# A new listed order for the first part of a linear-attention and two-layer MLP kernel, and two attention stages in some passes of block 2

## The chip, the cores and the metric

The kernel runs on one core of one Trainium2 chip. The metric is the device time of one execution in microseconds, as the median of three runs.

## The reference

Gated linear attention over 4 batches, 8 heads, 768 steps and a head width of 48, then two MLPs over the 3,072 tokens (width 384, hidden width 2,048), all in fp32:

```python
for t in range(S):
    state = alpha[:, :, t, :, None] * state + np.einsum('bhd,bhe->bhde', k[:, :, t], v[:, :, t])
    y[:, :, t] = np.einsum('bhd,bhde->bhe', q[:, :, t], state)
x = y.transpose(0, 2, 1, 3).reshape(B * S, H * D)
h = x @ w_in                                   # layer 1
g = np.where(h >= 1, h, np.where(h <= -1, 0.0, (h + 1) ** 2 / 4))
x = g @ w_out
h = x @ w_in2                                  # layer 2
g = h * np.clip(h + 3.0, 0.0, 6.0) / 6.0
out = g @ w_out2
```

## The kernel before

**Tiling.** Tokens lie along the free axis. There are 12 groups of 256 tokens, each with two halves of four heads: 24 attention units. Two groups make a block of 512 tokens; six blocks go through layer 1 and then through layer 2. The hidden width is cut into 16 steps f of 128. For each f, `mm1` makes a tile ph (3 x 3 matmuls of 128x128 by 128x512, because every fp32 operand is split into a high fp32r part and a low rest), ACT and DVE make the gate g from it, and `mm2` adds three output tiles po. Three ph buffers exist, one set of po, two buffers of ps_att for the attention, two x tiles and one more for block 2 (`turns`). The second product of a step is issued two steps behind the first (LAG).

**An attention unit** has stages that the listed order names by words: L and V load its data; p (scan of the gates), r (reciprocal), s (second scan), k (keys), R and Rc (queries) prepare it on DVE and ACT; T transposes the keys on TensorE and kt copies them; S makes the scores, m masks them on DVE; ST makes the chunk states, h, st and z sum and carry them; O makes the outputs into a ps_att tile, xc copies its high part into x on ACT, xl subtracts the low part on DVE (the last reader of the tile), mv moves 16 rows of each half head from a stage tile into x by six DMAs on POOL's queue, after both units of a group; gd is a range check on ACT that also ends the use of the loaded tile.

**Weights** come as 64-bit words of 768 KB a step: LW loads, ca (ACT), cb, cc, cd (DVE) turn them into fp32 in place, hi (ACT) and lo (DVE) split them. Words A, g, mx, gh, gl, B are the parts of a step of the MLP: A0_f is f of the first part of block 0, done with whole fp32 weights (`mm1_whole`, six recorded matmuls), A1 is block 1, A2 the rest of block 0; oc copies the three po tiles out. W n issues n filler matmuls that nobody reads.

**Order.** The string ORDER is run word by word, and a dependency added by hand keeps each engine's instructions in just that order: TensorE, DVE, ACT, POOL and SP (which issues the loads) are five queues that each run in the list's order. The list holds units 0 to 11, the preparation of unit 12, and the MLP up to block 0's last steps. Behind it (lines 753 to 804) a Python loop emits blocks 2 to 5 of layer 1 and all of layer 2. There the order on each engine is left to the scheduler that the program is compiled with. In layer 1 each pass f emits one `prep_step` (a third of a unit's preparation) and one `att_step` (a quarter of a unit: T and kt; S and m; ST, h, st and z; O, xc and gd, with xl, mv and the loads of the unit after next behind them). A block's four units are due before the block begins; blocks 2, 3 and 4 have 16 passes and so 16 attention stages each, units 12 to 23 in all. Blocks in the code are counted from 0.

The words L, T and so on are bound in `fns`; `load_qkv` places units 2, 3, 6 and 7 in weight tiles that are not used yet, and the others in a pool of two.

Of the kernel before, what the change touches and what calls it, by code (L numbers as in the profile page):

```python
# [38 lines left out]
ORDER = """
p0 r0 s0 L2 p1 k0 r1 T0 s1 W1 kt0 L3 ST0 k1 R1 T1 h0 Rc1 p2 st0 S1 kt1 z0 m1 ST1 p3 W8 LW1 R0 h1 Rc0 LW0 r3  # L40
st1 S0 s3 gd0 O1 m0 LW2 W1 xc1 k3 ca1 O0 r2 ca0 R3 W6 L4 cb1 xc0 z1 s2 Rc3 mv0 ca2 S3 k2 gd1 T2 m3 V2 W1 kt2
L5 R2 ST2 cc1 Rc2 T3 h2 kt3 p4 S2 st2 V3 ST3 m2 LW3 h3 O2 R4 st3 LW5 r4 s4 xc2 O3 Rc4 W1 k4 xc3 V4 cb0 ca3
S4 mv2 LW4 cc0 ca5 T4 m4 W2 kt4 V5 cd0 ST4 LW7 cb2 hi0 cd1 A0_0 ca4 cc2 LW6 hi1 cd2 sxh p5 A0_1 LW10 g0_0 z2
h4 cb3 A0_2 cc3 LW8 g0_1 mx0_0 cd3 gd4 LW9 B0_0 mx0_1 cb5 st4 z3 r5 s5 g0_2 A0_3 k5 gd3 mx0_2 cb4 O4 cc4 L7
g0_3 cd4 B0_1 cc5 ca7 cd5 gd2 B0_2 V6 mx0_3 xc4 L6 R5 Rc5 p7 ca6 S5 r7 hi2 s7 T5 hi3 L8 A0_5 R7 kt5 k7 Rc7
p6 ca8 A0_4 g0_5 m5 r6 ca9 s6 S7 g0_4 k6 ST5 m7 B0_3 ca10 mx0_4 mx0_5 h5 T6 R6 st5 B0_4 cb6 Rc6 cc6 gd5 cd6
kt6 O5 cb7 cc7 ST6 V7 xc5 xl4 L9 xl5 T7 h6 A0_6 mv4 kt7 lo0 st6 cd7 hi4 z6 ST7 lo1 gd6 lo2 S6 g0_6 h7 A0_7
m6 st7 mx0_6 hi6 z7 O7 p8 gd7 O6 V9 r8 xc7 s8 LW12 B0_5 g0_7 xl7 lo3 xc6 V8 mx0_7 B0_6 hi5 LW14 xl6 hi7 k8
mv6 ca12 lo6 LW13 B0_7 R8 lo4 Rc8 ca14 lo5 LW15 S8 oc0 cb9 cb8 A1_0 m8 LW11 ca13 cc8 A1_1 g1_0 lo7 cd8 A1_2
g1_1 mx1_0 cc9 A1_3 gh1_0 mx1_1 hi8 gl1_0 g1_2 lo8 B1_0 cd9 gh1_1 mx1_2 T8 gl1_1 gh1_2 A1_5 kt8 gl1_2 hi9  # L50
cb10 cc10 g1_3 ST8 cd10 B1_1 h8 hi10 mx1_3 st8 lo9 B1_2 gh1_3 z8 lo10 gd8 gl1_3 A1_4 ca11 cb12 cb11 g1_5
cc11 O8 cb13 A1_6 g1_4 mx1_5 L10 cc13 cd13 gh1_5 B1_3 ca15 mx1_4 gl1_5 gh1_4 V10 A1_7 xc8 gl1_4 cd11 g1_6
cc12 B1_4 g1_7 mx1_6 sxl A1_8 gh1_6 mx1_7 hi11 B1_5 gl1_6 gh1_7 lo11 g1_8 gl1_7 B1_6 cd12 mx1_8 hi12 p9 B1_7
gh1_8 gl1_8 r9 B1_8 s9 R9 A1_10 k9 Rc9 cb14 cc14 A1_11 g1_10 cd14 lo12 T9 mx1_10 hi13 A1_9 cb15 gh1_10 lo13
kt9 gl1_10 hi14 A1_13 cc15 g1_9 cd15 S9 lo14 ST9 mx1_9 hi15 m9 gh1_9 A1_12 gl1_9 h9 g1_11 B1_9 lo15 p10
g1_12 B1_10 mx1_11 R10 gh1_11 mx1_12 A1_14 st9 gl1_11 g1_13 z9 xl8 B1_11 r10 s10 gh1_12 gd9 O9 gl1_12 mx1_13
g1_14 B1_12 L11 k10 gh1_13 mx1_14 A1_15 gl1_13 gh1_14 Rc10 gl1_14 V11 xc9 B1_13 g1_15 xl9 mv8 p11 B1_14
mx1_15 r11 gh1_15 s11 A2_8 gl1_15 k11 B1_15 g2_8 R11 A2_9 oc1 mx2_8 gh2_8 A2_10 g2_9 gl2_8 B2_8 g2_10 mx2_9
S10 gh2_9 mx2_10 T10 gh2_10 m10 A2_12 kt10 Rc11 gl2_10 gl2_9 ST10 g2_12 T11 h10 B2_9 mx2_12 gd10 kt11 B2_10
gh2_12 st10 gl2_12 O10 ST11 V12 xc10 L12 xl10 A2_11 h11 st11 S11 g2_11 A2_13 m11 gd11 mx2_11 O11 p12 gh2_11  # L60
A2_14 V13 xc11 gl2_11 L13 xl11 g2_13 r12 mv10 B2_11 s12 g2_14 mx2_13 B2_12 k12 R12 gh2_13 Rc12 gl2_13 A2_15
mx2_14 gh2_14 gl2_14 g2_15 mx2_15 gh2_15 gl2_15 B2_13
"""
# [828 lines left out]
```

## Time and profile before

| | us |
|---|---|
| median of three runs (971.74 to 974.24) | 973.2 |
| profiled execution | 977.22 |
| its span, first to last instruction | 975.4 |
| TensorE busy / DVE busy / ACT busy | 930.7 / 532.3 / 530.7 |
| mean granted clock of TensorE | 0.976 |

Engines are written PE (TensorE), PEld (its weight loads), DVE, ACT, POOL and SP; SPq and ACTq are the queues that issue DMAs. Times count from the first instruction of the span. L120 is line 120 of the kernel; `ph<-x,w` is a tile written from two others by the program's names, with trailing numbers left out. A releaser is what ended the idle time before an instruction. The granted clock is given as a share of 2.4 GHz.

### The profile page before, as it was taken

The numbers are of one execution on the slowest core, as the hardware profiler recorded it, in microseconds if no ns is written. First come the engines' busy times: TensorE is split into PE (matmuls) and PEld (weight loads), VectorE is DVE, ScalarE is ACT, GpSimd is POOL, SyncE is SP. The second block draws the span as 40 slices with busy tenths as digits, with TensorE's granted clock in tenths as the row PEclk, the third lists the DMA queues.
The fourth block names the chain that finished last, engine by engine and source line by source line (L and its number), as shares of the span: only waits on it lengthen the run. The fifth ranks groups of instructions, "written<-read, shape, count | busy, mean of one in ns | idle before, by whom it ended". The sixth has DMA issues, their size and how long they took to land.

```text
span 975.4 us, 14259 instructions
## 1 busy us (share of the span) xinstructions
PE 930.7 (95%) x5786; PEld 736.0 (75%) x5790; DVE 532.3 (55%) x856; ACT 530.7 (54%) x855; POOL 39.5 (4%) x88
## 2 busy tenths in 40 slices
...
DMA packets 18026, 69.33 MB, mean 71 GB/s; under 512 B 3360, under 2 KB 3680, under 8 KB 15520
## 3 DMA queue, kind: packets, MB, share of 16 engines
...
q10 hardware_dynamic: 608, 0.62, 0.2%
q14 instruction: 27, 0.22, 0.1%
...
## 4 chain that ended last, share of the span: by engine, by line
PE 85%; DMA 5%; DVE 5%; ACT 3%; issue 1%; POOL 0%; SPq 0%; ACTq 0%; DVEq 0%
PE po L161 37%; PE ph L120 37%; PE ph L128 3%; PE ps_att L462 2%; DMA qkv_sb<-in_wgt 2%; PE ps_att L509 2%; PE ps_att L436 2%; PE ps_att L419 1%; DMA qkv_sb<-in_qkv 1%; PE po L134 1%; DMA x<-stage 1%; DVE w L113 1%; DMA xf<-stage 1%; DMA w<-in_qkv 1%; DVE R L446 1%
## 5 line engine op out<-in xcount | busy, mean ns | idle before, releaser
L161 PE MATMUL po<-g,w 128*128 128x512 f32 x1656 | 412.8, 393 | 0.0
L120 PE MATMUL ph<-x,w 128*128 128x512 f32 x1512 | 380.5, 397 | 12.2 <-DVE t L150 7.3
L161 PEld LDWEIGHTS po<-g,w 128*128 128x128 f32 x1656 | 308.7, 188 | 65.3
L120 PEld LDWEIGHTS ph<-x,w 128*128 128x128 f32 x1512 | 287.9, 191 | 74.1 <-DVE t L150 8.6
L786 DVE TENSOR_TENSOR g<-t,g 128x512 fp32r<-128x512 f32 x160 | 110.2, 691 | 95.0 <-ACT g L153 94.6
L153 ACT ACTIVATE g<-t 128x512 fp32r<-128x512 f32 x160 | 100.6, 631 | 104.6 <-DVE t L152 62.4
L152 DVE SCALAR_TENSOR_TENSOR t<-t,ph 128x512 f32<-128x512 f32 x96 | 66.1, 689 | 160.7 <-ACT t L145 160.7
L145 ACT ACTIVATE t<-ph,half 128x512 f32<-128x512 f32 x96 | 66.2, 689 | 158.1 <-PE ph L120 156.9
L140 ACT ACTIVATE t<-ph,half 128x512 f32<-128x512 f32 x96 | 65.7, 685 | 69.9 <-PE ph L120 61.8
L150 DVE TENSOR_TENSOR t<-t,ph 128x512 f32<-128x512 f32 x64 | 43.3, 681 | 47.8 <-ACT t L142 47.4
L142 ACT ACTIVATE t<-t 128x512 f32<-128x512 f32 x96 | 60.1, 630 | 2.3
L141 ACT ACTIVATE t<-t 128x512 f32<-128x512 f32 x96 | 60.1, 630 | 2.2
L120 PE MATMUL ph<-turns,w 128*128 128x512 f32 x144 | 36.3, 397 | 0.0
L550 POOL DMA_DIRECT2D x<-stage x48 | 24.0, 506 | 275.9 <-DVE rec L381 80.7
L374 DVE TENSOR_TENSOR_SCAN qkv_sb<-qkv_sb,zero 128x256 f32<-128x256 f32 x40 | 25.4, 677 | 16.1 <-DMA qkv_sb<-in_qkv 16.1
L446 DVE TENSOR_TENSOR R<-ps_att,mask 64x512 int32<-64x512 int32 x40 | 27.5, 688 | 11.0 <-PE ps_att L436 10.3
L462 PEld LDWEIGHTS ps_att<-qkv_sb,kt 64*64 64x64 f32 (+1 forms) x576 | 21.7, 142 | 15.1 <-issue 9.9
L462 PE MATMUL ps_att<-qkv_sb,kt 64*64 64x48 f32 (+1 forms) x576 | 25.9, 232 | 6.1 <-ACT kt L424 2.5
L120 PEld LDWEIGHTS ph<-turns,w 128*128 128x128 f32 x144 | 27.0, 188 | 6.2
L485 ACT ACTIVATE st<-sh 64x384 f32<-64x384 f32 x48 | 24.9, 519 | 7.7 <-DVE sh L478 6.6
L436 PEld LDWEIGHTS ps_att<-R,qkv_sb 64*64 64x64 f32 x640 | 21.4, 139 | 9.8 <-issue 5.5
L388 DVE TENSOR_TENSOR_SCAN qkv_sb<-qkv_sb,rec,zero 128x256 f32<-128x256 f32 x40 | 27.9, 739 | 0.7
...
## 6 DMA issues: line engine op xcount, KB each, us to landing
...
qkv_sb<-in_wgt SPq DMA_DIRECT2D x16, 768.0 KB, 4.2
w<-in_wgt SPq DMA_DIRECT2D x10, 768.0 KB, 9.5
st<-in_vst SPq DMA_DIRECT2D x44, 128.0 KB, 2.8
w<-in_qkv SPq DMA_DIRECT2D x4, 768.0 KB, 7.8
x<-in_wgt SPq DMA_DIRECT2D x4, 768.0 KB, 10.0
...
```

Source lines behind the costliest of these rows:

```text
L120: nc.tensor.matmul(ph, w[:, a, 0, j * P:(j + 1) * P], x[:, b, j], start=(i == 0), stop=(i == 3 * KD - 1))
L140: nc.scalar.activation(t, ph, AF.Relu, scale=-0.5, bias=half)
L141: nc.scalar.activation(t, t, AF.Relu, scale=-1.0, bias=1.0)
L142: nc.scalar.activation(t, t, AF.Square)
L145: nc.scalar.activation(t, ph, AF.Relu, scale=1.0 / 6.0, bias=half)
L150: nc.vector.tensor_tensor(out=t, in0=t, in1=ph, op=ALU.max)
L152: nc.vector.scalar_tensor_tensor(out=t, in0=t, scalar=1.0, in1=ph, op0=ALU.min, op1=ALU.mult)
L153: nc.scalar.activation(g[:, 0], t, AF.Copy)
L161: nc.tensor.matmul(po[m], w[:, a, 1, m * P:(m + 1) * P], g[:, b], start=(first and i == 0), stop=(last and i == 2))
L436: nc.tensor.matmul(ps[o0:o0 + C, r * NCH + c, :], n["kh"][p0:p0 + C, r, ks], R[p0:p0 + C, h, r, cs], start=True, stop=True,)
L462: nc.tensor.matmul(ps[C * h:C * h + C, c, r, :], n["kt"][k0:P, 2 * r + 1 - c // 2, C * h:C * h + C], n["v"][k0:P, 1 - c // 2, 2 * r + h, : ...
L786: nc.vector.tensor_tensor(out=g[:, 1], in0=tt, in1=g[:, 0].bitcast(F32), op=ALU.subtract)
```

## The change

The string ORDER is replaced by another with the same work and 35 fillers in eight places instead of 20 in seven. The loads of units 0, 1, 2, 3, 6 and 7 become three words each: Lp (the gates, 512 KB), Lk (the keys, 256 KB) and Lq (queries and values, 448 KB); before, unit 0 was loaded in those three parts, unit 1 whole and units 2, 3, 6 and 7 in two parts. The loads of the first two units, which stood ahead of the list, are words of it, and V0 and V1 are issued from SP instead of ACT. The tile of reciprocals is cut from a constant with four places instead of a pool of two. In the loop behind the list, passes 3, 7, 11 and 15 of block 2 emit two attention stages and two preparation steps instead of one. Of ORDER the diff below shows the lines that are spoken of further on.

```diff
 ORDER = """
-p0 r0 s0 L2 p1 k0 r1 T0 s1 W1 kt0 L3 ST0 k1 R1 T1 h0 Rc1 p2 st0 S1 kt1 z0 m1 ST1 p3 W8 LW1 R0 h1 Rc0 LW0 r3
...
-S4 mv2 LW4 cc0 ca5 T4 m4 W2 kt4 V5 cd0 ST4 LW7 cb2 hi0 cd1 A0_0 ca4 cc2 LW6 hi1 cd2 sxh p5 A0_1 LW10 g0_0 z2
-h4 cb3 A0_2 cc3 LW8 g0_1 mx0_0 cd3 gd4 LW9 B0_0 mx0_1 cb5 st4 z3 r5 s5 g0_2 A0_3 k5 gd3 mx0_2 cb4 O4 cc4 L7
-g0_3 cd4 B0_1 cc5 ca7 cd5 gd2 B0_2 V6 mx0_3 xc4 L6 R5 Rc5 p7 ca6 S5 r7 hi2 s7 T5 hi3 L8 A0_5 R7 kt5 k7 Rc7
-p6 ca8 A0_4 g0_5 m5 r6 ca9 s6 S7 g0_4 k6 ST5 m7 B0_3 ca10 mx0_4 mx0_5 h5 T6 R6 st5 B0_4 cb6 Rc6 cc6 gd5 cd6
-kt6 O5 cb7 cc7 ST6 V7 xc5 xl4 L9 xl5 T7 h6 A0_6 mv4 kt7 lo0 st6 cd7 hi4 z6 ST7 lo1 gd6 lo2 S6 g0_6 h7 A0_7
-m6 st7 mx0_6 hi6 z7 O7 p8 gd7 O6 V9 r8 xc7 s8 LW12 B0_5 g0_7 xl7 lo3 xc6 V8 mx0_7 B0_6 hi5 LW14 xl6 hi7 k8
-mv6 ca12 lo6 LW13 B0_7 R8 lo4 Rc8 ca14 lo5 LW15 S8 oc0 cb9 cb8 A1_0 m8 LW11 ca13 cc8 A1_1 g1_0 lo7 cd8 A1_2
...
-kt9 gl1_10 hi14 A1_13 cc15 g1_9 cd15 S9 lo14 ST9 mx1_9 hi15 m9 gh1_9 A1_12 gl1_9 h9 g1_11 B1_9 lo15 p10
-g1_12 B1_10 mx1_11 R10 gh1_11 mx1_12 A1_14 st9 gl1_11 g1_13 z9 xl8 B1_11 r10 s10 gh1_12 gd9 O9 gl1_12 mx1_13
...
+Lp0 Lk0 Lp1 p0 Lq2 r0 s0 Lq0 p1 Lq1 k0 Lk1 R0 T0 r1 Lp2 Lk2 Rc0 s1 kt0 S0 R1 ST0 Lq3 k1 Rc1 m0 W4 Lp3 Lk3 p2
...
+O2 m3 ca4 p4 O3 xc2 gd2 W9 r4 s4 V4 xc3 V5 hi0 mv2 k4 Lq6 R4 T4 cb4 W2 LW3 kt4 p5 Rc4 ST4 cb1 S4 LW5 h4 cc1
+gd4 W7 m4 st4 Lp6 Lk6 cd1 ca3 O4 r5 hi1 A0_0 cb2 L8 cc2 xc4 ca5 xl4 cd2 sxh A0_1 p6 LW7 g0_0 cb5 s5 A0_2
+g0_1 V6 mx0_0 LW6 p8 B0_0 ca7 mx0_1 g0_2 r8 LW10 cb3 cc3 B0_1 ca6 mx0_2 LW9 cd3 hi2 k5 hi3 A0_3 z3 R5 gd3
+LW8 cc4 Rc5 cd4 ca9 B0_2 Lp7 Lk7 cc5 g0_3 cd5 R6 Lq7 T5 ca8 mx0_3 S5 kt5 r6 p7 Rc6 A0_4 ca10 R7 r7 Rc7 s7
...
+LW13 hi5 O7 z7 mx0_5 gd7 p9 T8 V9 B0_5 xc7 R9 LW11 kt8 xl7 g0_6 lo2 mv6 ST8 lo5 LW12 g0_7 mx0_6 S8 h8 B0_6
+m8 st8 Rc9 z8 mx0_7 gd8 lo0 O8 hi6 r9 B0_7 s9 L10 hi4 ca13 k9 ca11 lo4 A1_0 oc0 lo6 V10 cb9 LW15 cb10 A1_1
...
+cd10 A1_8 gl1_5 hi10 xl8 g1_7 lo10 S9 cb13 ST9 g1_8 m9 B1_5 h9 mx1_7 st9 cd12 A1_10 gh1_7 z9 gl1_7 gd9 mx1_8
...
 """
...
@@ -337,27 +338,32 @@
         for _ in range(n):
             nc.tensor.matmul(ph, filler[:, 0:P], filler, start=True, stop=True)
 
-    def load_qkv(u, eng=nc.sync):
+    def load_qkv(u, part=None):
         g, hf = u
         i = units.index(u)
-        if i in (2, 3, 6, 7):
-
-            ta, tb = (wp.tile([P, 6 * AG], F32, name=f"w{NF - 2 * (i % 4 - 2) - k}") for k in (1, 2))
-            parts = [(ta, 0, 6 * AG), (tb[:, 0:QKV_W - 6 * AG], 6 * AG, QKV_W)]
-        else:
-            t = a2.tile([P, QKV_W], F32, name="qkv_sb")
-            ta, tb = t[:, 0:6 * AG], t[:, 6 * AG:]
-            parts = [(t, 0, QKV_W)]
-            if i == 0:
-                parts = [(t[:, a:b], a, b) for a, b in ((0, 4 * AG), (4 * AG, 6 * AG), (6 * AG, QKV_W))]
-        for t, a, b in parts:
-            eng.dma_start(out=t, in_=qkv[g, hf, :, a:b])
-        qa = ta.rearrange("p (a r t) -> p a r t", a=3, r=2)
-        un[u].update({
-            "both": qa[:, 0:2], "P": qa[:, 0], "gam": qa[:, 1], "kh": qa[:, 2],
-            "q": tb[:, 0:2 * AG].rearrange("p (r t) -> p r t", r=2),
-            "v": tb[:, 2 * AG:2 * AG + 8 * D].rearrange("p (n h e) -> p n h e", n=2, h=4),
-        })
+        n = un[u]
+        if "ta" not in n:
+            if i in (2, 3, 6, 7):
+
+                ta, tb = (wp.tile([P, 6 * AG], F32, name=f"w{NF - 2 * (i % 4 - 2) - k}") for k in (1, 2))
+                tb = tb[:, 0:QKV_W - 6 * AG]
+            else:
+                t = a2.tile([P, QKV_W], F32, name="qkv_sb")
+                ta, tb = t[:, 0:6 * AG], t[:, 6 * AG:]
+                n["t"] = t
+            qa = ta.rearrange("p (a r t) -> p a r t", a=3, r=2)
+            n.update({
+                "ta": ta, "tb": tb, "both": qa[:, 0:2], "P": qa[:, 0], "gam": qa[:, 1], "kh": qa[:, 2],
+                "q": tb[:, 0:2 * AG].rearrange("p (r t) -> p r t", r=2),
+                "v": tb[:, 2 * AG:2 * AG + 8 * D].rearrange("p (n h e) -> p n h e", n=2, h=4),
+            })
+        if part is None:
+            nc.sync.dma_start(out=n["t"], in_=qkv[g, hf])
+        for k, (t, a, b) in enumerate((
+            (n["ta"][:, 0:4 * AG], 0, 4 * AG), (n["ta"][:, 4 * AG:], 4 * AG, 6 * AG), (n["tb"], 6 * AG, QKV_W)
+        )):
+            if part == k:
+                nc.sync.dma_start(out=t, in_=qkv[g, hf, :, a:b])
 
     def load_v(u, eng=nc.sync):
         g, hf = u
@@ -377,7 +383,7 @@
 
     def recip(u):
         n = un[units[u]]
-        n["rec"] = a2.tile([P, 2], F32, name="rec")
+        n["rec"] = recs[:, 2 * (u % 4):2 * (u % 4) + 2]
         nc.vector.tensor_scalar(out=n["rec"], in0=n["P"][:, :, AG - 1], scalar1=LEAST, scalar2=None, op0=ALU.max)
         nc.vector.reciprocal(out=n["rec"], in_=n["rec"])
 
@@ -556,6 +562,7 @@
         n = un[units[u]]
         nc.scalar.activation(n["both"], n["both"], AF.Abs, accum_out=guard[:, u:u + 1])
 
+    recs = const.tile([P, 8], F32, name="recs")
     x_parts = {}
     prep_n = [3 * (READY + 1)]
     att_n = [4 * READY]
@@ -714,7 +721,8 @@
         nc.vector.tensor_tensor(out=x_t[0][:, 1], in0=xf, in1=x_t[0][:, 0].bitcast(F32), op=ALU.subtract)
 
     fns = {
-        "L": lambda u: load_qkv(units[u]), "V": lambda u: load_v(units[u]),
+        "L": lambda u: load_qkv(units[u]), "Lp": lambda u: load_qkv(units[u], 0), "Lk": lambda u: load_qkv(units[u], 1),
+        "Lq": lambda u: load_qkv(units[u], 2), "V": lambda u: load_v(units[u]),
         "p": prefix, "r": recip, "s": gammas, "k": keys, "R": queries, "Rc": queries_2,
         "T": transposes, "kt": keys_t, "S": scores, "m": masked, "ST": states, "h": sums, "st": states_2,
         "z": state_on, "O": outputs, "xc": x_high, "xl": x_low, "mv": x_moves, "gd": ranges,
@@ -738,12 +746,8 @@
 
     start = len(nc.cur_bb.bb.instructions)
 
-    load_qkv(units[0])
     nc.scalar.dma_start(out=cst_sb, in_=cst)
     nc.scalar.dma_start(out=mask, in_=msk)
-    load_v(units[0], nc.scalar)
-    load_qkv(units[1])
-    load_v(units[1], nc.scalar)
     for word in ORDER.split():
         name = word.rstrip("0123456789_")
         fns[name](*(int(n) for n in word[len(name):].split("_") if n))
@@ -766,7 +770,8 @@
             w = w_t[layer * NF + f]
             mm1(nc, ph, w, x_t[layer * NBLK + bi])
 
-            if layer == 0:
+            na = 0 if layer else 2 if bi == 2 and t % 4 == 3 else 1
+            for _ in range(na):
                 prep_step(att_n[0] // 4 + 2)
             if last1 and f == LAG:
                 w_load(NF + 2)
@@ -777,7 +782,7 @@
             tt = t_p.tile([P, NB], F32, name="t")
             gate_a(nc, layer, ph, tt, half)
             run_deferred()
-            if layer == 0:
+            for _ in range(na):
                 att_step()
             g = g_p.tile([P, 2, NB], F32R, name="g")
             gate_b(nc, layer, ph, tt, g)
```

## Rows read from the trace of the kernel before

**Rows 1.** Page, part 1: busy us of TensorE (share of the span), instructions.
```profile
PE 930.7 (95%) x5786; PEld 736.0 (75%) x5790; DVE 532.3 (55%) x856; ACT 530.7 (54%) x855; POOL 39.5 (4%) x88
```

**Rows 2.** Windows by stage: us, busy (instructions) by engine, PEclk, DMA share, GB/s.
```profile
0.00:49.20 49.20, 33.89 (x501) 23.85 (x505) 38.48 (x75) 21.91 (x36) 8.50 (x22) 0.91 0.88 302
49.20:123.20 74.00, 61.82 (x452) 33.23 (x452) 53.53 (x92) 47.28 (x77) 6.37 (x14) 0.89 0.51 177
...
322.00:417.00 95.00, 93.29 (x734) 73.94 (x732) 54.14 (x98) 58.43 (x101) 8.35 (x18) 0.98 0.23 75
417.00:504.40 87.40, 85.93 (x649) 67.33 (x646) 47.66 (x82) 56.37 (x97) 5.99 (x12) 0.98 0.18 58
504.40:570.00 65.60, 63.23 (x271) 51.48 (x269) 47.95 (x65) 53.22 (x83) 0.00 (x0) 0.97 0.34 120
```

**Rows 3.** Windows of three stretches, columns as in rows 2.
```profile
47.40:54.20 6.80, 5.02 (x6) 2.19 (x7) 4.38 (x9) 3.16 (x3) 0.00 (x0) 0.50 1.01 387
74.70:81.50 6.80, 3.79 (x8) 2.26 (x9) 4.97 (x9) 2.12 (x3) 0.00 (x0) 0.50 0.27 111
122.50:129.30 6.80, 6.03 (x14) 4.79 (x15) 0.00 (x0) 2.64 (x4) 0.00 (x0) 0.50 0.31 125
```

**Rows 4.** Waits of TensorE over the span: us in total, times, longest us.
```profile
PE ph L120 <- DVE t L150: 7.3, 4, 2.4
PE ps_att L419 <- DVE rec L381: 5.4, 1, 5.4
PE ph L120 <- DMA x<-stage: 4.9, 1, 4.9
...
PE ps_att L462 <- ACT kt L424: 3.2, 3, 2.2
PE ph L128 <- DMA xf<-stage: 2.1, 1, 2.1
PE ps_att L462 <- DVE R L446: 1.9, 1, 1.9
```

**Rows 5.** Timeline of DVE, first 20 us: start, us, what [idle before].
```profile
4.67 1.27 DVE L374 TENSOR_TENSOR_SCAN qkv_sb<-qkv_sb,zero 128x256 f32<-128x256 f32 x2 [3.24 <-DMA qkv_sb<-in_qkv]
...
6.39 1.40 DVE L388 TENSOR_TENSOR_SCAN qkv_sb<-qkv_sb,rec,zero 128x256 f32<-128x256 f32 x2
11.61 1.27 DVE L374 TENSOR_TENSOR_SCAN qkv_sb<-qkv_sb,zero 128x256 f32<-128x256 f32 x2 [3.83 <-DMA qkv_sb<-in_qkv]
12.80 0.67 DVE L395 TENSOR_TENSOR qkv_sb<-qkv_sb 128x512 f32<-128x512 f32 x1
```

**Rows 6.** Page, part 6: DMA issues, KB each, median us to landing.
```profile
w<-in_wgt SPq DMA_DIRECT2D x10, 768.0 KB, 9.5
st<-in_vst SPq DMA_DIRECT2D x44, 128.0 KB, 2.8
```

**Rows 7.** Chain that ended last, 40 to 125 us: start, us, what.
```profile
42.24 6.56 DMA xf<-stage
...
114.51 8.51 DMA x<-stage
```

**Rows 8.** Timeline of TensorE, first 50 us, columns as in rows 5.
```profile
21.56 1.67 PE L338 MATMUL ph<-filler 128*128 128x512 bf16 x7 [0.16 <-issue]
...
25.29 1.25 PE L509 MATMUL ps_att<-R,st 128*64 128x64 f32 x32
```

**Rows 9.** Timeline at the starts of block 5 and of the second layer.
```profile
500.94 1.99 POOL L550 DMA_DIRECT2D x<-stage  x4 [18.98 <-DVE x L540]
...
504.36 4.24 PE L120 MATMUL ph<-x,w 128*128 128x512 f32 x18
...
510.24 1.28 DVE L150 TENSOR_TENSOR t<-t,ph 128x512 f32<-128x512 f32 x2 [8.49 <-ACT t L142]
...
510.98 5.30 PE L120 MATMUL ph<-x,w 128*128 128x512 f32 x15 [2.37 <-DVE t L150]
...
571.87 3.29 PE L120 MATMUL ph<-x,w 128*128 128x512 f32 x9 [1.75 <-DVE t L150]
```

More of the change, by code (lines that the diff above doesn't have):

```diff
@@ L39 @@
 ORDER = """
-p0 r0 s0 L2 p1 k0 r1 T0 s1 W1 kt0 L3 ST0 k1 R1 T1 h0 Rc1 p2 st0 S1 kt1 z0 m1 ST1 p3 W8 LW1 R0 h1 Rc0 LW0 r3
-st1 S0 s3 gd0 O1 m0 LW2 W1 xc1 k3 ca1 O0 r2 ca0 R3 W6 L4 cb1 xc0 z1 s2 Rc3 mv0 ca2 S3 k2 gd1 T2 m3 V2 W1 kt2
-L5 R2 ST2 cc1 Rc2 T3 h2 kt3 p4 S2 st2 V3 ST3 m2 LW3 h3 O2 R4 st3 LW5 r4 s4 xc2 O3 Rc4 W1 k4 xc3 V4 cb0 ca3
-S4 mv2 LW4 cc0 ca5 T4 m4 W2 kt4 V5 cd0 ST4 LW7 cb2 hi0 cd1 A0_0 ca4 cc2 LW6 hi1 cd2 sxh p5 A0_1 LW10 g0_0 z2
-h4 cb3 A0_2 cc3 LW8 g0_1 mx0_0 cd3 gd4 LW9 B0_0 mx0_1 cb5 st4 z3 r5 s5 g0_2 A0_3 k5 gd3 mx0_2 cb4 O4 cc4 L7
@@ L50 @@
[L50 to L54, printed above, removed]
@@ L55 @@
-kt9 gl1_10 hi14 A1_13 cc15 g1_9 cd15 S9 lo14 ST9 mx1_9 hi15 m9 gh1_9 A1_12 gl1_9 h9 g1_11 B1_9 lo15 p10
-g1_12 B1_10 mx1_11 R10 gh1_11 mx1_12 A1_14 st9 gl1_11 g1_13 z9 xl8 B1_11 r10 s10 gh1_12 gd9 O9 gl1_12 mx1_13
-g1_14 B1_12 L11 k10 gh1_13 mx1_14 A1_15 gl1_13 gh1_14 Rc10 gl1_14 V11 xc9 B1_13 g1_15 xl9 mv8 p11 B1_14
-mx1_15 r11 gh1_15 s11 A2_8 gl1_15 k11 B1_15 g2_8 R11 A2_9 oc1 mx2_8 gh2_8 A2_10 g2_9 gl2_8 B2_8 g2_10 mx2_9
-S10 gh2_9 mx2_10 T10 gh2_10 m10 A2_12 kt10 Rc11 gl2_10 gl2_9 ST10 g2_12 T11 h10 B2_9 mx2_12 gd10 kt11 B2_10
@@ L60 @@
-gh2_12 st10 gl2_12 O10 ST11 V12 xc10 L12 xl10 A2_11 h11 st11 S11 g2_11 A2_13 m11 gd11 mx2_11 O11 p12 gh2_11
-A2_14 V13 xc11 gl2_11 L13 xl11 g2_13 r12 mv10 B2_11 s12 g2_14 mx2_13 B2_12 k12 R12 gh2_13 Rc12 gl2_13 A2_15
-mx2_14 gh2_14 gl2_14 g2_15 mx2_15 gh2_15 gl2_15 B2_13
+Lp0 Lk0 Lp1 p0 Lq2 r0 s0 Lq0 p1 Lq1 k0 Lk1 R0 T0 r1 Lp2 Lk2 Rc0 s1 kt0 S0 R1 ST0 Lq3 k1 Rc1 m0 W4 Lp3 Lk3 p2
+T1 W6 kt1 R2 V1 h0 Rc2 V0 r2 S1 LW1 s2 ST1 m1 st0 W1 LW2 h1 O0 k2 st1 p3 T2 V2 xc0 LW0 kt2 R3 O1 r3 ca2 s3
+ST2 xc1 V3 Rc3 mv0 k3 S2 LW4 ca1 z1 z0 W2 h2 gd0 cb0 T3 m2 ca0 L4 W4 kt3 cc0 gd1 ST3 cd0 st2 S3 h3 L5 z2 st3
@@ new lines @@
+O2 m3 ca4 p4 O3 xc2 gd2 W9 r4 s4 V4 xc3 V5 hi0 mv2 k4 Lq6 R4 T4 cb4 W2 LW3 kt4 p5 Rc4 ST4 cb1 S4 LW5 h4 cc1
+gd4 W7 m4 st4 Lp6 Lk6 cd1 ca3 O4 r5 hi1 A0_0 cb2 L8 cc2 xc4 ca5 xl4 cd2 sxh A0_1 p6 LW7 g0_0 cb5 s5 A0_2
+g0_1 V6 mx0_0 LW6 p8 B0_0 ca7 mx0_1 g0_2 r8 LW10 cb3 cc3 B0_1 ca6 mx0_2 LW9 cd3 hi2 k5 hi3 A0_3 z3 R5 gd3
+LW8 cc4 Rc5 cd4 ca9 B0_2 Lp7 Lk7 cc5 g0_3 cd5 R6 Lq7 T5 ca8 mx0_3 S5 kt5 r6 p7 Rc6 A0_4 ca10 R7 r7 Rc7 s7
+ST5 g0_4 k7 A0_5 h5 mx0_4 gd5 m5 st5 B0_3 s6 g0_5 s8 S7 k8 O5 m7 B0_4 V7 xc5 R8 L9 xl5 Rc8 k6 mv4 cb7 T6 cc7
@@ new lines @@
+S6 kt6 cd7 ST6 m6 A0_7 h6 cb6 st6 cc6 T7 cd6 O6 kt7 z6 lo3 gd6 ST7 V8 lo1 xc6 LW14 A0_6 h7 hi7 xl6 st7 lo7
+LW13 hi5 O7 z7 mx0_5 gd7 p9 T8 V9 B0_5 xc7 R9 LW11 kt8 xl7 g0_6 lo2 mv6 ST8 lo5 LW12 g0_7 mx0_6 S8 h8 B0_6
+m8 st8 Rc9 z8 mx0_7 gd8 lo0 O8 hi6 r9 B0_7 s9 L10 hi4 ca13 k9 ca11 lo4 A1_0 oc0 lo6 V10 cb9 LW15 cb10 A1_1
+g1_0 cc10 p10 A1_2 g1_1 mx1_0 cb8 cb15 A1_3 gh1_0 mx1_1 ca15 gl1_0 cc15 g1_2 A1_4 cd15 cc8 gh1_1 T9 ca12
+mx1_2 B1_0 gl1_1 kt9 gh1_2 cd8 g1_3 B1_1 gl1_2 cb12 cc12 g1_4 A1_5 mx1_3 cc9 hi8 mx1_4 A1_6 gh1_4 lo8 gh1_3
```

10 lines of the change are left out of this document (added).

## The prediction

> **What bounds the kernel now.** I read the busy shares first. TensorE is busy for 930.7 of 975.4 us [rows 1], so at most 44.7 us of the span are idle on the engine that does most of the work, and by the table of stages 27.5 of those lie in the first 123.2 us (49.2 - 33.9 and 74 - 61.8), where the listed order runs [rows 2]. The table shows where the clock is lost as well. A mean granted clock c over a stretch of T means (1 - c) x 2 x T at the lower level, 1.2 GHz, and half of that is lost if TensorE has work. By stage: 0 to 49.2, 0.09 x 49.2 = 4.4 us; 49.2 to 123.2, 0.11 x 74 = 8.1; the stretches of blocks 3, 4 and 5, 1.9, 1.7 and 2.0. In the second stage no engine is near full: TensorE 61.8, DVE 53.5 and ACT 47.3 of 74 us. That is a stage of waits. Three of the low stretches are rows of their own, 6.8 us each at half of full speed, 3.4 us lost each [rows 3].
>
> The table of TensorE's waits names the rest [rows 4]: 7.3 us in four waits for DVE's max (t L150), which frees a ph buffer; 5.4 in one, put down to a reciprocal; 4.9 and 2.1 for the moves of rows into x and xf; 3.2 for ACT copies and 1.9 for a masking inside the attention.
>
> **Start.** DVE's timeline shows its first scan at 4.67 us and unit 1's scan at 11.61, after 3.83 us of idling for that unit's load [rows 5]. k0 and T0 stand behind p1, so TensorE gets its first transposes only after it. In the list of before, unit 1 comes as one load of 1,216 KB behind the 1,216 KB of unit 0; now Lp1 (512 KB) stands third, behind 768 KB. The bytes up to its end fall from 2,432 to 1,280 KB. At the mean 302 GB/s of the stage [rows 2] these 1,152 KB are 3.9 us, more than the 3.83 us of idling. R0 (0.7 us, like k0 in the row at 12.80) now stands between k0 and T0 and needs Lq0, so I take 3.0 us; bounds 0 (DVE is nearly saturated later anyway) and 3.8.
>
> Six loads become eighteen where there were twelve. Each costs SP an issue of some 0.4 us, on a queue that mostly waits. Were their latencies in series, the nearest row is the load of a v half, 128 KB in 2.8 us [rows 6]: 6 x 2.8 = 16.8 us. They are issued ahead of use and several at a time, so I take 0 and keep 16.8 for a rival. The Trainium skill, "DMA: Bandwidth & Descriptors", section "Anatomy of one DMA — SWDGE (gpsimd) path", speaks against splitting: it gives about 2.0 us fixed for each DMA whatever its size. By that rule as an estimate the six would cost 12 us in series. The page measured another issuing path, and no run here shows the sum.
>
> V0 and V1 go from ACT's queue to SP's; behind Lk3 they have 5 MB ahead, 16.5 us at 302 GB/s, and O0 and O1 use them only after about 20 us of DVE work. Cost 0; if they were late, O0 and everything behind it on TensorE's queue would wait. The reciprocal's tile moved to a constant with four places: the same instructions, cost 0.
>
> **The moves into xf (A0_0).** The chain shows the last moves in flight for 6.56 us from 42.24 [rows 7], and TensorE waits 2.1 us for them after 2.2 us for an ACT copy (the longest of the 3.2) [rows 4]. Between mv2 and A0_0 the list of before has T4, ST4 and W2 on TensorE; the new one has T4, ST4, S4, O4 and 9 fillers. S4 and O4 are 32 small matmuls each, 1.2 us each at full clock [rows 8], and are taken from later places: 2.4 us that need not be done after A0_0. Avoidable: 2.1 + 2.2 idle and 3.4 us of the clock from 47.4 to 54.2 [rows 3], 7.7. Taken 3.5, since DVE is busy 38.5 of 49.2 us and its work before A0_0 is 2.5 us longer (z2, p5, r5, h4 and cb4 against cb2). The fifteen additional fillers are 0.24 us each [rows 8], 3.6 us, and hidden where TensorE would wait; if those gaps close, they cost 3.6.
>
> **The output tile held (T5).** ps_att has two buffers. O4's is held until x_low(4), and in the list of before xl4 stands behind ST6. So S5, T5, ST5 share one buffer, and T5 waited 5.4 us for m5, just ahead of the reciprocal that the table names [rows 4]; the low stretch from 74.7 to 81.5 follows [rows 3]. In the new list xl4 comes nine words after O4, before any T or S; O5 to xl5, O6 to xl6 have at most one attention step between. The later wait for a masking (1.9 us, at ST9) has the same cause, xl8 late, and xl8 now stands before S9. Avoidable in the second stage: 5.4 of wait and 5.1 of clock (8.1 less the first low stretch's part, 2.5, and the last half microsecond); 10.5 in all, and 1.9 for ST9. I take 4 and 1.5. Why so little: DVE has 92 us of work before 123.2 [rows 2] and the new list puts unit 9's key chain ahead of A1_0 too, about 4.4 us (p9 1.27, s9 1.40, k9 and R9 0.67 each, and two small ones) [rows 5]. With the start at 4.67 us, DVE alone holds A1_0 to at least about 100 us; a gap closed on TensorE is a gap gained only while DVE has slack.
>
> **The moves into x (A1_0).** In flight 8.51 us from 114.51, because loads of weights share the DMA engines [rows 7]. TensorE waits 4.9 us [rows 4], then loses 3.4 at the lower clock from 122.5 on [rows 3]: 8.3. Between mv6 and A1_0 before: B0_7 and S8. Now: ST8, S8, B0_6, O8, B0_7, twice B's six matmuls and three attention steps, over 8 us of work, about the length of the moves. The new list puts LW12, L10 behind mv6 where there were LW13, LW15 and LW11, so the moves are not freer. Taken 4 of 8.3.
>
> **Two stages in one pass.** At the start of block 5 the last four moves go out at 500.94 [rows 9]; TensorE does the j = 0 matmuls of three ph early, then the other 18 in one piece from 504.36, so all three gates finish late: DVE only at 510.24, and TensorE idles 2.37 us because the three ph buffers are full. It restarts at half the clock. Blocks 3 and 4 do the same. The four waits sum to 7.3 [rows 4]; the fourth, 1.75 at 571.87 [rows 9], is at the start of the second layer, where no attention is left, and stays. So 5.6 idle, and 1.7 us of clock each (the 1.9, 1.7 and 2.0 above hold little else), 5.1: 10.7. With two attention stages in steps 3, 7, 11 and 15 of block 2, unit 15's outputs come in its step 12 and not 15, some 15 us before block 3, and blocks 4 and 5 keep four stages of lead. Taken 10. The same matmuls are only done sooner; block 2's DVE and ACT have room (54.1 and 58.4 of 95 us in block 3, whose steps are the same) [rows 2]. If a double pass stalled like block 5's start, it would cost 2.4 + 1.7 us, four of them 16.4.
>
> **Sum.** 3.0 + 3.5 + 4 + 1.5 + 4 + 10 = 26.0. The profiled execution took 977.2 us, 4.0 above the median of 973.2. 977.2 - 26.0 = 951.2 there, 947.2 as a median. All avoidable losses of the list are 3.8 + 7.7 + 10.5 + 1.9 + 8.3 = 32.2; with the 10.7 the least time is 930.
>
> **Rivals.** (1) Only the tail gains: the listed part's gaps turn up elsewhere, since DVE, its loads in series (16.8 us) or the fillers (3.6) fill what was freed. Then 973.2 - 10 = 963. For it: DVE's load; against: its own idle time, 10.7 us of the first 49.2 and 20.5 of the next 74. (2) Only the list gains, since the passes with two stages stall as priced: 973.2 - 16 = 957 with new stalls equal to the old. Against: the room just named. (3) Slower: L8 now stands on SP's queue ahead of LW7, LW6, LW10, LW9, LW8; before, it stood behind all five. A weight load takes 9.5 us to land [rows 6] and ca7, ca6 and ca9 stand on ACT 3 to 5 us behind their loads. With ACT waiting there, the gates wait, then TensorE: three times 9.5 + 3.4 us of clock, 39 us, less 26, gives 986. It decides from 26 us of such waits on, about two full ones. Against: DMA moved 177 GB/s in that stage and 302 in the one before [rows 2], so the queue was not full. (4) No change: the terms balance.
>
> **Chances and range.** Both gains as summed 0.62, rival 1 0.22, rival 2 0.05, rival 3 0.07, no change 0.04. A difference under 0.3% (2.9 us) can't be told from none in this kernel. Faster 0.89, same 0.04, slower 0.07. The range runs from near the least time to rival 1's with 2 us: 933 to 965.
>
> **What would show it.** Right: first transposes near 10 us; no wait for xf's or x's moves over 1 us; no 5 us wait at T5; A1_0 near 110 and the list's end some 16 us sooner; blocks 3, 4, 5 starting with no idle TensorE and clock 1.0. Wrong: ACT waiting for weights between 50 and 80 us; new low-clock stretches inside block 2; DVE without idle time up to A1_0 and A1_0 still near 120.

## The result, and the profile after

The changed kernel takes 934.7 us (median; 933.0 to 935.5) against 973.7 us (971.7 to 974.2): a ratio of 0.960, 95% interval 0.958 to 0.962, so 39.0 us less. The forecast was 947, the range 933 to 965. The profiled execution took 933.0 us, with a span of 931.1 (975.4 before) and a mean granted clock of 0.996 (0.976). The chip, the reference and the computation are the same.

TensorE's waits, in the same view as [rows 4] (us in total, times, longest us). Line numbers have moved by one or more: L121 is the old L120, L425 the old L419.

```profile
PE ps_att L468 <- ACT kt L430: 2.5, 2, 2.2
PE ps_att L515 <- DVE sh L480: 1.8, 1, 1.8
...
PE ph L129 <- DVE w L96: 1.3, 1, 1.3
PE ps_att L425 <- DVE qkv_sb L401: 1.3, 2, 1.0
...
PE ph L121 <- DVE t L151: 0.4, 1, 0.4
```

The 5.4 us ahead of a transpose and the waits for both moves of rows are gone, and so are all four waits for DVE's max (7.3 us). The 0.4 us in the last line stand at another place: ahead of the last ph of block 5, before the second layer begins at 525.66 (TensorE's timeline; in brackets the wait ahead of a piece).

```profile
521.44 2.34 PE L121 MATMUL ph<-x,w 128*128 128x512 f32 x9 [0.40 <-DVE t L151]
523.62 2.20 PE L162 MATMUL po<-g,w 128*128 128x512 f32 x9
525.66 1.30 PE L121 MATMUL ph<-x,w 128*128 128x512 f32 x5
```

What remains is at most 2.2 us at one place, and all of it but that 0.4 lies in the first 61 us.

The windows, as [rows 2], cut at the changed kernel's own stages: up to A0_0, from there to A1_0, block 2, block 5.

```profile
0.00:45.60 45.60, 36.25 (x547) 25.18 (x552) 38.36 (x79) 23.87 (x41) 8.57 (x22) 0.96 0.92 321
45.60:104.70 59.10, 57.79 (x488) 31.88 (x488) 54.15 (x94) 46.39 (x75) 6.68 (x14) 1.00 0.68 233
...
211.90:298.10 86.20, 86.20 (x749) 69.24 (x748) 54.90 (x102) 56.89 (x98) 6.01 (x12) 1.00 0.24 79
461.10:525.70 64.60, 64.20 (x283) 52.24 (x282) 45.77 (x64) 51.72 (x82) 0.00 (x0) 1.00 0.29 98
```

A0_0 is at 45.6 us (49.2 before), A1_0 at 104.7 (123.2), block 2 at 211.9 (238.0), the second layer at 525.7 (565.9), the last matmul ends at 923.6 (967.5). So the listed part gives 26.1 of the 44 us between the two traces, blocks 2 to 5 give 14.1, and the second layer 3.7. (The trace of before is of an execution 3.5 us over its median; between the medians there are 39.0 us.) In the stage from A0_0 to A1_0 TensorE is now busy 57.8 of 59.1 us instead of 61.8 of 74, at a clock of 1.00 instead of 0.89; DVE does the same 54 us of work and is at 92%.

The start, on DVE's timeline (as [rows 5]): unit 1's scan follows unit 0's chain with no wait, at 7.72 us instead of 11.61.

```profile
4.70 1.27 DVE L380 TENSOR_TENSOR_SCAN qkv_sb<-qkv_sb,zero 128x256 f32<-128x256 f32 x2 [3.27 <-DMA qkv_sb<-in_qkv]
...
7.72 1.25 DVE L380 TENSOR_TENSOR_SCAN qkv_sb<-qkv_sb,zero 128x256 f32<-128x256 f32 x2
8.89 0.66 DVE L401 TENSOR_TENSOR qkv_sb<-qkv_sb 128x512 f32<-128x512 f32 x1
```

The start of block 5, on TensorE's timeline (compare [rows 9]): the first product of block 5 begins at 461.09, first and second products alternate, and nothing waits.

```profile
459.05 2.20 PE L162 MATMUL po<-g,w 128*128 128x512 f32 x9
461.09 2.20 PE L121 MATMUL ph<-x,w 128*128 128x512 f32 x9
463.13 2.20 PE L162 MATMUL po<-g,w 128*128 128x512 f32 x9
465.17 2.20 PE L121 MATMUL ph<-x,w 128*128 128x512 f32 x9
```

The moves of rows are little faster. These are the DMA issues between 85 and 106 us (KB, median us to landing), where the last six moves ahead of A1_0 are issued:

```profile
x<-stage POOLq DMA_DIRECT2D x6, 32.0 KB, 7.3
```

They take 7.3 us in the median (8.51 for the one in [rows 7]), under the work that now stands between them and A1_0.

### The profile page after: what moved, and what is told of

The parts are those of the page before. It is cut to its first block, busy times and chain, and to the rows that moved or that the text cites. A ratio compares the mean times of both kernels' runs of the same rounds, so it can differ in the third digit from the quotient of the medians.

```text
span 931.1 us, 14299 instructions
## 1 busy us (share of the span) xinstructions
PE 912.6 (98%) x5800; PEld 726.3 (78%) x5805; DVE 530.9 (57%) x856; ACT 531.2 (57%) x855; POOL 40.3 (4%) x88
## 4 chain that ended last, share of the span: by engine, by line
PE 89%; DMA 5%; DVE 4%; ACT 1%; issue 1%; SPq 0%; DVEq 0%; ACTq 0%
PE po L162 39%; PE ph L121 38%; PE ps_att L515 2%; PE ps_att L468 2%; DMA qkv_sb<-in_wgt 2%; PE ps_att L442 2%; PE po L135 2%; PE ph L129 2%; DMA x<-in_wgt 1%; DMA qkv_sb<-in_qkv 1%; PE ps_att L425 1%; DVE w L114 0%; DVE qkv_sb L90 0%; DVE qkv_sb L380 0%; DVE qkv_sb L394 0%
## 5 line engine op out<-in xcount | busy, mean ns | idle before, releaser
L121 PE MATMUL ph<-x,w 128*128 128x512 f32 x1512 | 370.6, 390 | 0.4 <-DVE t L151 0.4
L121 PEld LDWEIGHTS ph<-x,w 128*128 128x128 f32 x1512 | 282.9, 188 | 60.7 <-DVE t L151 1.2
L121 PE MATMUL ph<-turns,w 128*128 128x512 f32 x144 | 36.9, 396 | 0.0
L121 PEld LDWEIGHTS ph<-turns,w 128*128 128x128 f32 x144 | 26.8, 188 | 6.1
L394 DVE TENSOR_TENSOR_SCAN qkv_sb<-qkv_sb,recs,zero 128x256 f32<-128x256 f32 x40 | 27.8, 737 | 0.6
L515 PEld LDWEIGHTS ps_att<-R,st 128*64 128x64 f32 x640 | 20.8, 138 | 9.2 <-issue 4.2
L515 PE MATMUL ps_att<-R,st 128*64 128x64 f32 x640 | 23.6, 225 | 2.4 <-DVE sh L480 1.8
```

The lines of the kernel that those rows point to most:

```text
L121: nc.tensor.matmul(ph, w[:, a, 0, j * P:(j + 1) * P], x[:, b, j], start=(i == 0), stop=(i == 3 * KD - 1))
L515: nc.tensor.matmul(ps[C * h:C * h + C, r, cs], s[:, h, r, c, :], R[:, h, r, cs], start=True, stop=True)
```

## The experiments

All ratios are to the kernel before, timed beside each on the same chip. The profiles of lists that are the same up to A0_0 differ by up to 3 us in when A0_0 starts (45.6 to 48.6 in seven runs), so differences of 2 us between two variants are at the edge of what these medians tell.

### The two parts of the change, each alone

The old list with the new passes:

```diff
-            if layer == 0:
+            na = 0 if layer else 2 if bi == 2 and t % 4 == 3 else 1
+            for _ in range(na):
                 prep_step(att_n[0] // 4 + 2)
...
-            if layer == 0:
+            for _ in range(na):
                 att_step()
```

> The old list, with two attention stages in four passes of block 2. By the theory of the prediction (a block's rows were moved too late; four stages of lead end that) the three waits of 1.5 to 2.4 us and their low-clock stretches at the starts of blocks 3, 4 and 5 go: 10 to 14 us less than before, about 960 to 964 us, and the listed part stays as it was (block 2 begins near 238 us). If the block starts wait for another reason (the order that the scheduler gives the three ph tiles), the waits stay and the time is 973 to 974. The wait at the start of the second layer is open: if it goes here too, it belongs to this part, and the time is some 3 us lower.

959.0 us, ratio 0.985 (0.983 to 0.987): 15.2 us less. TensorE's longest waits are those of the listed part, and the row of waits for t L150 with 7.3 us is not among them:

```profile
PE ps_att L419 <- DVE qkv_sb L395: 5.0, 1, 5.0
PE ps_att L419 <- DVE rec L381: 4.3, 1, 4.3
PE ph L120 <- DMA x<-stage: 4.0, 1, 4.0
```

Blocks 3, 4 and 5 start without a wait, and the 1.75 us at the start of the second layer is gone too. A wait of 0.6 us is left, at 537.4 us, inside block 5.

The new list with one stage a pass:

```diff
-            na = 0 if layer else 2 if bi == 2 and t % 4 == 3 else 1
+            na = 0 if layer else 1
```

> The new list, with one attention stage in every pass as before. If the two parts of the change add up, block 2 begins near 212 us and the time is 934.7 plus 10 to 14 us, 945 to 949, with the waits at the starts of blocks 3, 4 and 5 back. If the new list alone gave most of it and the tail's waits were a follow-up of the listed part, the time is 935 to 938. If the wait at the start of the second layer comes back as well, it belongs to the passes with two stages.

952.6 us, ratio 0.979 (0.977 to 0.981): 21.5 us less. Block 2 begins at 213.9 us, and the waits at the starts of blocks 3, 4 and 5 are back at their old sizes (1.71, 1.48 and 2.37 us), as is the one at the second layer (1.85). A wait of 1.23 us inside block 5 and one of 1.48 for moves of rows, ahead of block 3's second ph, are new:

```profile
PE ph L121 <- DVE t L151: 8.6, 5, 2.4
...
PE ph L121 <- DMA x<-stage: 1.5, 1, 1.5
```

15.2 and 21.5 make 36.7 of the 39.0 us, so the two parts add up nearly whole. One thing differs from the prediction's account: in this trace none of these waits is followed by a low clock. The wait of 2.37 us ahead of block 5's fourth ph, on TensorE's timeline, and the window behind it (the column ahead of the DMA share is the granted clock):

```profile
486.00 4.38 PE L121 MATMUL ph<-x,w 128*128 128x512 f32 x18 [2.37 <-DVE t L151]
```

```profile
486.00:490.00 4.00, 4.00 (x18) 3.30 (x19) 1.93 (x4) 3.75 (x7) 0.00 (x0) 1.00 0.00 0
```

### Which block start gives what

```diff
-            na = 0 if layer else 2 if bi == 2 and t % 4 == 3 else 1
+            na = 0 if layer else 2 if bi == 4 and t % 4 == 3 else 1
```

> The new kernel with its two-stage passes in block 4 instead of block 2: blocks 3 and 4 start without a lead, block 5 with one. If each block's start has its own price, the waits at the starts of blocks 3 and 4 stay as in the run with the new list alone (952.6) and only block 5's part is saved: 2.4 to 4.1 us, 948 to 950. If the wait at the start of the second layer follows from block 5's late start, it goes too: 945 to 948. If the second layer's wait comes from somewhere else, it stays at 1.8 us.

943.8 us, ratio 0.970 (0.967 to 0.972): 8.8 us less than the new list alone, more than either expectation. The waits at blocks 3 and 4 stay (1.71 and 1.47), that of block 5 goes, and that of the second layer goes with it. The third wait in the row is one of 0.67 us inside block 5, at 524.3 us; the second layer begins at 537.1:

```profile
PE ph L121 <- DVE t L151: 3.9, 3, 1.7
```

So block 5 and the second layer hang together. In the old trace the first three ph of block 5 come out late and in one bunch [rows 9]; what this shifts so that the second layer waits some 60 us later was not tried.

Half the lead:

```diff
-            na = 0 if layer else 2 if bi == 2 and t % 4 == 3 else 1
+            na = 0 if layer else 2 if bi == 2 and t % 8 == 7 else 1
```

> The new kernel with two attention stages in passes 7 and 15 of block 2 only, so a lead of two stages and not four. If the block starts only need their rows moved in time (moves land some 2 us after their issue there), two passes of 5 us are enough: 934 to 936, no waits at the starts of blocks 3 to 5. If the lead has to be a whole unit, waits of 1 to 2 us come back: 938 to 944.

934.7 us, ratio 0.959 (0.956 to 0.961), the same as four stages of lead, with no wait at any block start. Two stages, about two passes of 5 us, are enough for moves that land in time.

### The held output tile, alone

Two words of the old list moved, nothing else:

```diff
-... mx0_3 xc4 L6 ... xc5 xl4 L9 ... A1_7 xc8 gl1_4 ... z9 xl8 B1_11 ...
+... mx0_3 xc4 xl4 L6 ... xc5 L9 ... A1_7 xc8 xl8 gl1_4 ... z9 B1_11 ...
```

> The old kernel with two words of its list moved: xl4 from behind xc5 to right behind xc4, and xl8 from behind z9 to right behind xc8, so that the ps_att tiles of O4 and O8 are free sooner. If the held tile is what made T5 wait 5.4 us and ST9 1.9, both waits go, the low-clock stretch behind T5 goes or gets shorter, and the time is 4 to 9 us under before, 965 to 970. If T5 waits because DVE is late in any case, its wait only changes its name and the time is 972 to 975.

960.5 us, ratio 0.985 (0.982 to 0.988): 13.4 us less, where 4 to 9 were expected. The waits of 5.4 (T5) and 1.9 us (ST9) are gone from the table of waits, and those for the moves and at the block starts stay:

```profile
PE ph L120 <- DVE t L150: 7.9, 5, 2.4
...
PE ps_att L462 <- ACT kt L424: 3.7, 3, 2.7
PE ph L120 <- DMA x<-stage: 3.6, 1, 3.6
```

A1_0 begins at 112.3 us instead of 123.3, ahead of the second word's place, so most of the gain is the first word's; the two were not tried one by one. The low stretches behind T5 and at 88 us are gone too; only the one at A1_0 is left of those three, and it is half as long.

### Does DVE set the pace?

The prediction took less than half of what it called avoidable, because DVE would fill the freed time. Ten instructions of DVE that nobody needs, spread from A0_0 to A1_0, in either list:

```diff
+        "X": lambda: nc.vector.memset(filler, 1.0),
```

(The ten words X in the list are left out here.)

> The same ten instructions in the old list, from A0_0 to A1_0. The prediction held back half of the listed part's gain because DVE would fill the freed time. If DVE has slack in that stretch of the old kernel (it is busy 53.5 of 74 us and the waits are TensorE's), they cost under 1.5 us: 973 to 975. If DVE was in truth on the path there, 977 to 979.

> The new kernel with ten additional DVE instructions that nobody needs (a memset of the filler tile, 0.49 us each by its row in the trace of before) spread over the list from A0_0 to A1_0, 4.9 us in all. If DVE sets the pace in that stretch now, most of it comes back in the time: 938 to 940. If TensorE does, which has no wait over 0.3 us there after 60 us, 935 to 936.5.

In the old list 974.3 us, ratio 0.999 (0.997 to 1.001): no cost that shows. In the new one 936.6, ratio 0.962 (0.960 to 0.963), 1.9 us over the changed kernel by the medians, with intervals that overlap (0.958 to 0.962). The stage is 61.3 us there, 59.2 in the changed kernel and 58.0 to 60.3 in four traces of the new list. The windows from A0_0 to A1_0, old list first (DVE's busy time is the third number of the row's engines):

```profile
49.10:122.20 73.10, 62.17 (x452) 33.09 (x453) 57.11 (x103) 48.09 (x77) 6.37 (x14) 0.89 0.51 178
```

```profile
47.00:108.40 61.40, 58.81 (x493) 32.14 (x489) 57.39 (x104) 45.49 (x73) 6.67 (x14) 1.00 0.65 222
```

DVE was no bound in the old stage. In the new one, where it is busy for 54 of 59 us, the additional work probably costs a part of its 4.9 us, but one or two us are not clear of the noise.

Four of DVE's subtractions on POOL:

```diff
+        eng = nc.gpsimd if i in (1, 2, 3, 5) else nc.vector
-        nc.vector.tensor_tensor(out=w[:, 1], ...)
+        eng.tensor_tensor(out=w[:, 1], ...)
```

> The new kernel with the subtractions of the words lo1, lo2, lo3 and lo5 on POOL, which is idle 96% of the time, instead of DVE: 3.8 us of DVE's work less in the stretch from A0_0 to A1_0, in which DVE is now busy 94%. If DVE sets the pace there and POOL does the four in the time that the list leaves, 931 to 934. If POOL is several times slower, or the moves behind it on its queue come late, TensorE waits for weights or moves: 936 to 945.

936.9 us, ratio 0.962 (0.960 to 0.964), no gain. (DVE's share in that stage is 92%, not the 94% of the expectation.) POOL takes 1.86 us for each, DVE 0.95. A wait of 2.2 us for DVE begins at 89.7 us, ahead of an A0 step, which the changed kernel does not have; what makes DVE late there was not traced. POOL's row:

```profile
L713 POOL TENSOR_TENSOR w<-w,w 128x768 fp32r<-128x768 f32 x4 | 7.4, 1861 | 0.0
```

### The loads, the fillers and the cover

The loads in the pieces of before (unit 1 whole), all issued at the word Lp:

```diff
-        if part is None:
+        if part is None or (part == 0 and i == 1):
             nc.sync.dma_start(out=n["t"], in_=qkv[g, hf])
...
+        elif part == 0:
+            pieces = ((n["ta"], 0, 6 * AG), (n["tb"], 6 * AG, QKV_W))
...
-        ... "Lk": lambda u: load_qkv(units[u], 1),
-        "Lq": lambda u: load_qkv(units[u], 2), ...
+        ... "Lk": lambda u: None,
+        "Lq": lambda u: None, ...
```

> The new kernel with the loads of units 0, 1, 2, 3, 6 and 7 in the pieces of before (unit 0 in three, unit 1 whole, the others in two), each issued at its first word. By the theory of the prediction unit 1's scan waits until about 11.6 us again, the first transposes until 13.5, and DVE, which is nearly saturated behind it, carries 3 us of that to the end: 937 to 939 us. If a later wait hides it, 934 to 936. If the more numerous pieces cost time, 930 to 934.

939.1 us, ratio 0.963 (0.961 to 0.966), 4.4 us slower than the changed kernel by the medians and 3.0 by the ratios. Unit 1's scan waits 1.83 us for its load on DVE's timeline and starts at 9.64, not at 11.6, and A0_0 is at 51.1:

```profile
9.64 1.27 DVE L381 TENSOR_TENSOR_SCAN qkv_sb<-qkv_sb,zero 128x256 f32<-128x256 f32 x2 [1.83 <-DMA qkv_sb<-in_qkv]
```

No fillers (each W of the list left out):

> The new kernel without the 35 listed fillers, the rest as it is. If the fillers fill time in which TensorE would wait and only hold its clock, leaving them out costs the low-clock stretches that come back: one to three of up to 3.4 us lost, 936 to 943 us. If the fillers delay what stands behind them (35 at 0.24 us are 8.4 us of TensorE's queue), the time falls to 929 to 934.

936.7 us, ratio 0.962 (0.960 to 0.964), some 2 us slower by the medians, which is at the edge of the noise. The clock up to A0_0 falls from 0.96 to 0.72, and A0_0 starts at 49.9 us, but most of TensorE's work there is small matmuls between waits:

```profile
0.00:49.90 49.90, 37.86 (x517) 30.16 (x517) 39.28 (x80) 25.35 (x42) 8.53 (x22) 0.72 0.89 309
```

Fillers in the old list, 20 ahead of T5 and 18 ahead of A1_0:

```diff
-... s7 T5 ... cb9 cb8 A1_0 ...
+... s7 W20 T5 ... cb9 cb8 W18 A1_0 ...
```

> The old kernel with 20 fillers ahead of T5 and 18 ahead of A1_0, in its two longest waits of the listed part (5.4 and 4.9 us). The waits stay, only the clock is held. If half of the time of the low-clock stretches behind them is lost, as the sum of the prediction had it, up to 3.4 us for each, the time is 967 to 971. If the stretches cost nothing because other engines set the pace there, 973 to 975; if the fillers are longer than the waits, up to 978.

970.9 us (966.4 to 972.5), ratio 0.996 (0.994 to 0.998): 3.0 us less, of up to 6.8 that two low stretches were priced at. The trace is of the fastest execution, 4.4 us under the median. In its window from A0_0 to A1_0 the clock is 0.97 instead of 0.89; the time in which TensorE has no other work stays, filled:

```profile
49.50:117.60 68.10, 65.68 (x489) 34.76 (x491) 53.64 (x93) 47.89 (x77) 6.37 (x14) 0.97 0.54 190
```

Less cover for the moves into x:

```diff
-... mv6 ST8 lo5 ... mx0_6 S8 h8 B0_6 m8 st8 Rc9 z8 mx0_7 gd8 lo0 O8 ... A1_0 oc0 ...
+... mv6 lo5 ... mx0_6 B0_6 Rc9 mx0_7 lo0 ... A1_0 ST8 S8 h8 m8 st8 z8 gd8 O8 oc0 ...
```

> The new kernel with ST8, S8, h8, m8, st8, z8, gd8 and O8 moved from ahead of A1_0 to right behind it: 3.3 us of TensorE's work less between the last moves into x and the matmuls that read them. The moves take some 7 us there, and B0_6 and B0_7 cover 5. By the theory of the prediction TensorE waits 2 to 5 us ahead of A1_0 and loses up to 3.4 more at the lower clock: 937 to 943. If the moves are no longer what A1_0 waits for, 934 to 936.

944.3 us, ratio 0.969 (0.966 to 0.972), 9.6 us slower, a little over the range, but not for the reason given. TensorE's timeline shows only 0.79 us of waiting for the moves at A1_0; the large waits are for DVE, ahead of B0_6 (1.42) and, behind A1_0, for the max that frees a ph (3.91):

```profile
97.82 5.42 PE L134 MATMUL po<-g,x 128*128 128x512 f32 x12 [1.42 <-DVE g L683]
104.03 2.29 PE L120 MATMUL ph<-x,w 128*128 128x512 f32 x9 [0.79 <-DMA x<-stage]
...
119.48 2.08 PE L120 MATMUL ph<-x,w 128*128 128x512 f32 x4 [3.91 <-DVE t L685]
```

The attention work moved behind A1_0 delays the gates that stand behind it on DVE. So this run shows what the place of that work is worth, and does not settle how much of it is cover for the moves; that B0_6 and B0_7 alone leave 0.8 us uncovered, it does show.

## Why the prediction was right, and where it was off

**Direction and mechanisms.** The forecast was 26 us, the gain is 39.0. Both parts act, as forecast, and add up (36.7). The time fell inside the range because the range reaches down to near the least time of the sum, 930: of the 42.9 us that the prediction called avoidable nearly all came, where it took 26.0. Rival 1 (only the tail gains, 963) falls with the new list alone, which gives 21.5 us; rival 2 (the passes with two stages stall) with the new passes alone, which give 15.2 us and no stall. Loads in series would have made the split dearer, and the pieces of before are 4.4 us slower. The slower case came in small. The chain that ended last, of the changed kernel from 30 to 62 us (start, us, what), has a weight load behind L8 on the path:

```profile
42.97 12.83 DMA x<-in_wgt
...
55.82 0.02 ACT x L79
...
56.68 0.67 ACT t L141
...
58.70 0.69 DVE g L684
59.39 0.88 DVE w L96
...
60.31 1.99 PE ph L129 x4
```

That is LW7, issued 0.4 us behind L8. ca7 waits for it on ACT, and through the gate TensorE waits 1.3 us ahead of an A0 step, once, not 9.5 + 3.4 us three times: the loads behind it were out before 50 us and had landed when they were needed.

**Start, 3.0.** First transposes at 9.61 us ("near 10"). The run with the pieces of before puts the split at 3.0 to 4.4 us, so the size holds. Not all of the earlier scan is the split's, though: with the pieces of before, unit 1's scan still starts 2.0 us sooner than in the old kernel (9.64 and 11.61). There the halves of V0 and V1 were loading beside it, from ACT's queue; that they now come behind it was priced at 0, and no run separates the two. The fixed cost of about 2.0 us for each DMA, which the Trainium skill gives in "DMA: Bandwidth & Descriptors", section "Anatomy of one DMA — SWDGE (gpsimd) path", does not show as a price for each more: the first five loads that SP issues in the changed kernel are 0.45 to 0.49 us apart and take 3.9 to 6.3 us to land, so they overlap. What one of them costs by itself no run here shows.

**The moves into xf, 3.5.** No run isolates this term. The waits of 2.1 and 2.2 us ahead of A0_0 are gone, and the low stretch from 47.4 us with them. The reading of the lists has a slip: S4 stands ahead of mv2 in the list of before, so it was done before A0_0 in both, and only O4, 1.2 us and not 2.4, is taken from a later place. A0_0 is 3.6 us earlier in the profiled run; over the traces it is at 45.6 to 48.6 us in seven and was at 49.1 to 50.6 in five with the old list. If the parts of the list add up, which no run tests, 3.7 to 5.1 of its 21.5 us are left for the moves into xf and those into x together, where 3.5 and 4 were forecast.

**The output tile held, 4 + 1.5.** This is the term that was mis-sized most. Moving two words alone gives 13.4 us. The prediction had the mechanism and the avoidable sum, 10.5 + 1.9 = 12.4, and cut it to 5.5 with the argument that DVE fills what TensorE frees. Its own bound did not ask for that: DVE holds A1_0 to "at least about 100 us", and with two words moved A1_0 was still at 112.3; it came at 104.7 in the changed kernel, and at 106.6 to 108.7 in three other traces of its list. The ten idle instructions show the slack as well: 4.9 us of additional work on DVE have no cost that shows in the old stage. Summed busy time says where a stage could end at the earliest; it was used as if it had said that half the gain is lost.

**The moves into x, 4.** The wait of 4.9 us at A1_0 is gone. With the tile fixed alone, 3.6 us of it stay, so the new order removes it and not the tile; how much is cover in the narrow sense stays open.

**Two stages in one pass, 10.** 15.2 alone. The three block starts lost their waits as forecast. One step failed: that the fourth wait, at the start of the second layer, "stays". Its 1.75 us are gone in every trace in which block 5 starts with a lead, and the second layer is 3.7 us shorter. The rest was sized too small because the prediction priced idle time and the clock alone. These are the windows of blocks 2 to 5, from the first product of block 2 to that of the second layer, in the old kernel, with the new list alone, and in the changed kernel (417.0 and 504.4 us in [rows 2] are some 7 us behind the starts of blocks 4 and 5):

```profile
237.98:565.88 327.90, 322.34 (x2314) 256.56 (x2312) 197.41 (x334) 220.01 (x369) 18.34 (x38) 0.98 0.23 76
213.88:541.20 327.32, 319.04 (x2314) 253.36 (x2313) 195.63 (x332) 218.64 (x368) 18.34 (x38) 1.00 0.23 76
211.85:525.66 313.81, 313.42 (x2314) 252.76 (x2313) 193.99 (x331) 220.89 (x368) 18.36 (x38) 1.00 0.24 78
```

TensorE has the same number of instructions in each. Of the 14.1 us between the first row and the third, 5.2 are idle time and 8.9 are busy time. About 3.3 of these 8.9 go with the clock (322.3 against 319.0, where no clock was lost), and 5.1 were priced. The other 5.6 are in no term of the prediction: at a clock of 1.00 the same work takes TensorE 319.0 us with one stage a pass and 313.4 with the lead. What in the order makes it slower is not shown; as the ends of matmuls are modelled, idle and busy time divide only roughly. The double passes cost nothing that shows in block 2 (no wait, clock 1.00).

**Fillers.** Priced at 0 where they fill waits. Without them the kernel is 2.0 us slower by the medians, at the edge of the noise: nothing shows that they cost time, and that they gain some is not clear.
